# A fused attention and two-MoE kernel: later logits, transposes first, weight blocks and returning weights laid out and timed anew

## The chip, the cores and the metric

One core of a Trainium2 chip runs the whole program. The metric is the device time of one execution in microseconds (us); lower is better. The time before is the median of three runs.

## The reference, cut to what matters

Block-causal attention (8 batches, 8 heads, 576 positions, head size 64, blocks of 64) gives 4608 tokens of 512 numbers. They pass a first MoE layer (one expert, squared ReLU, 512 to 2048 to 512) and a second, soft one (32 slots).

```python
attn = softmax(where(block_i >= block_j, q @ k.T / 8, -1e9)) @ v
x = attn.transpose(0, 2, 1, 3).reshape(4608, 512)
h = np.maximum(x @ w_in, 0.0)             # 512 x 2048
x = h * h @ w_out                         # 2048 x 512
logits = x @ phi                          # 512 x 32
d = softmax over tokens(logits);  slot_input = d.T @ x
slot_out[e] = relu(slot_input[e] @ w1[e]) @ w2[e]      # 8 experts, 4 slots each
out = softmax over slots(logits) @ slot_out
```

## The kernel before, in words

**Chunks and slots.** The tokens are cut into 12 chunks of 384. The first MoE layer is cut into 16 blocks `ft` of 128 hidden columns. A slot is one chunk with one block: `slot_h` (line 885) makes the hidden values in the accumulator bank `HB` with 12 matmuls of 384 columns at line 899, and `slot_o` (line 912) adds their product with `w_out` into the three `O` banks with 9 matmuls of 512 columns at line 924. Each number is split into a high and a low part, so that three matmuls stand for one. There are 192 slots; chunk c covers the slots 16c to 16c+15 (chunks 0 and 1 share their slots in another order).

**Weights.** `W[ft]` holds the high part of a block, its first 512 columns of `w_in` and its last 512 of `w_out`. The low parts lie in DRAM (`wlo_d`) and come back through a ring of six tiles, `WL`, one 512 KB load a slot (line 890).

**Three fast stretches.** Chunks 4 and 5, 7 and 8, 9 and 10 are done in pairs by `fast` (line 1186). Sums and differences of the inputs (`combos`, line 1026, on VectorE and ScalarE) and of the weights let 7 products (`product`, line 1132, matmuls at line 1140) stand for 8. A fast stretch takes 32 slots: 8 pair loops over two blocks, each with 7 products and two `o_block` calls (line 1156, matmuls at 1168) for the second chunk's first half of the work, then a row of 16 `o_block` calls for the other chunk. The weight operands of the products pass through a ring in the first halves of `W[0]` to `W[7]`, filled by `w_entry` (line 1115); the combined inputs lie in `EX`, in the first halves of `W[8]` to `W[15]` and in `WL`. So after the first and the third fast stretch the first halves of all 16 `W` must return before chunks 6 and 11 are done in the plain way: line 1269 reads them from `whi_d`.

**Weight operands in DRAM.** Before the fast stretches, `prep` (line 1000) forms sums of the blocks for each of 8 pairs p, at the slots that `PREP` names (24 to 54), and stores their high and low parts in `ws_d` (lines 1022 and 1023), where a row of 512 numbers holds 256 of the high and 256 of the low part. Four of the seven operands are read from there (line 1128, one DMA). The other three are plain halves of blocks: line 1125 reads 128 KB from `whi_d`, line 1126 reads 128 KB from `wlo_d`, in rows of 1 KB. `whi_d` is written in the slots of chunk 2 (line 1471).

**The second layer's first half.** When a chunk's `O` banks close, they are copied to `X2`, and `moe2` (line 1280) runs for that chunk. For the 8 chunks numbered 2 to 9 in order of closing, VectorE transposes `X2` in 32x32 blocks into `XB` (line 1299), a DMA stores `XB` in DRAM (line 1302), and four DMAs read it back transposed into `YA` (line 1305). Then PE makes the logits (line 1331); a maximum, two exponentials, two small transposes (line 1361) and the product of the weights with `X2` (line 1384) follow, and the result is added into `acc`. `next(g_)` emits the part up to the DMAs when the chunk closes; the rest is emitted later, by `send(s)`, and its first matmul is tied to the first matmul of slot s (line 1334). That slot is the closing slot + 4 (lines 1193 and 1478). In a fast stretch's row of `o_block` calls, a slot number covers two calls.

**Attention.** Batches 0 and 1 are done at the start. For batches 2 to 7 `job64` (line 426) does two heads at a time, 24 jobs in all: scores in three phases (line 462), maxima on VectorE (472), exponentials on ScalarE (479), the joining of half rows (486 to 499), scaling (505, 506), transposes on VectorE (509), and the product with `v` (517, 72 matmuls). The jobs are spread over the slots by due times, `JOBS` (line 1435): first slot, and slots per job.

**What sets the order.** `Program.order` (line 99) is a planner: each step has costs, a due time and steps that it follows; a simulated clock picks, engine by engine, the ready step with the smallest due time, and the program is emitted in that order. `after` ties a step to others that must be placed before it. All DMAs go out on one queue, SP's, in that order; the queue stops at a DMA whose semaphores are not there yet. Four of the eight PSUM banks (`w`) are shared by attention, the odd products and the second layer.

Line 466 says when a job's first score matmul may be placed: after the factors (`fct`) of the job before are computed, so ahead of that job's product with `v`.

```python
after=() if i != ph_[0] else oldF + (fct_at if ph_ is PHASES[0] and fct_at else pv_end)
```

## Time and profile before

| | |
|---|---|
| median of three runs | 1192.55 us (1192.54 to 1194.65) |
| the profiled execution's own time | 1187.98 us |
| its span, first to last instruction | 1186.2 us |
| granted TensorE clock, mean | 0.989 |
| PE (matmul) busy | 1134.9 us, 96% |
| VectorE (DVE) busy | 864.6 us, 73% |
| ScalarE (ACT) busy | 641.4 us, 54% |
| DMA queue q1 | 259.54 MB, 67.2% of 16 engines |

Busy time is the time in which an engine had an instruction under way. Matmuls are pipelined, so a busy PE may still do less than it could; idle time of PE, and what ended it, is the more telling number. A row of the waits says which engine and line waited for which other, the total in us, how often, and the longest. A row of the timeline gives start and duration in us, then engine, line, operation and shape, merged over consecutive instructions of the same kind, and in brackets the idle time before it and what ended it. SPq is the DMA queue's own sequencer.

### The profile page before, as it was taken

The numbers are of one execution on the slowest core, as the hardware profiler recorded it, in microseconds if no ns is written. First come the engines' busy times: TensorE is split into PE (matmuls) and PEld (weight loads), VectorE is DVE, ScalarE is ACT, GpSimd is POOL, SyncE is SP. The second block draws the span as 40 slices with busy tenths as digits, with TensorE's granted clock in tenths as the row PEclk, the third lists the DMA queues.
The fourth block names the chain that finished last, engine by engine and source line by source line (L and its number), as shares of the span: only waits on it lengthen the run. The fifth ranks groups of instructions, "written<-read, shape, count | busy, mean of one in ns | idle before, by whom it ended". The sixth has DMA issues, their size and how long they took to land.

```text
span 1186.2 us, 28720 instructions
## 1 busy us (share of the span) xinstructions
PE 1134.9 (96%) x10918; PEld 931.5 (79%) x10918; DVE 864.6 (73%) x2469; ACT 641.4 (54%) x2041; POOL 4.1 (0%) x17
## 2 busy tenths in 40 slices
PE   5899999999999899999999999999999999899995
PEld 4677787878888788888877788788888899689843
DVE  7999988987778776887889777877896766532202
ACT  6888787667566466545566655646562000122324
POOL 1000000000000000000000000000000000000000
PEclk9899899999999999999999999999999999999998
DMA  7699547745555854665586653756564966997889
GB/s 232 200 340 292 179 154 265 242 166 184 183 180 186 251 173 138 189 198 179 173 261 238 218 177 95 224 187 192 179 185 140 292 206 191 360 374 249 295 329 320
DMA packets 145642, 261.37 MB, mean 220 GB/s; under 512 B 19680, under 2 KB 75232, under 8 KB 145504
## 3 DMA queue, kind: packets, MB, share of 16 engines
q1 hardware_dynamic: 145504, 259.54, 67.2%
q8 instruction: 86, 1.41, 0.5%
q14 instruction: 52, 0.43, 0.1%
HBM read 222.78 MB, written 36.70 MB: 219 GB/s over the span
## 4 chain that ended last, share of the span: by engine, by line
PE 77%; DVE 10%; DMA 7%; ACT 4%; issue 2%; SPq 0%; DVEq 0%; ACTq 0%
PE O L1168 16%; PE HB L899 14%; PE O L924 13%; PE HB L1140 9%; PE B L1140 6%; PE B L462 6%; PE B L517 5%; DMA WL<-wlo_d 3%; DMA YA<-xt_d 1%; PE B L1724 1%; DVE anm L645 1%; PE B L1331 1%; PE B L1384 1%; PE O L1688 1%; ACT aF L479 1%
## 5 line engine op out<-in xcount | busy, mean ns | idle before, releaser
L479 ACT ACTIVATE aF<-B,aF 128x192 f32<-128x192 f32 (+8 forms) x432 | 165.9, 418 | 51.5 <-DVE aF L474 38.3
L924 PE MATMUL O<-W,MG 128*128 128x512 f32 x600 | 178.1, 400 | 1.0 <-DVE MG L908 1.0
L1168 PE MATMUL O<-W,MG 128*128 128x512 f32 x576 | 167.8, 399 | 1.0 <-ACT X L1173 0.6
L899 PE MATMUL HB<-MX,W 128*128 128x384 f32 x544 | 148.8, 345 | 1.7 <-ACT R L905 1.7
L472 DVE TENSOR_REDUCE aF<-B 128x1 f32<-128x192 f32 (+8 forms) x432 | 109.7, 314 | 34.5 <-PE B L462 33.6
L924 PEld LDWEIGHTS O<-W,MG 128*128 128x128 f32 x600 | 110.2, 188 | 20.2 <-issue 1.9
L1168 PEld LDWEIGHTS O<-W,MG 128*128 128x128 f32 x576 | 106.0, 188 | 23.8 <-issue 1.7
L899 PEld LDWEIGHTS HB<-MX,W 128*128 128x128 f32 x544 | 98.6, 189 | 7.5 <-ACT R L905 2.6
L509 DVE STREAM_TRANSPOSE aF<-aF 128x256 f32<-128x256 f32 (+8 forms) x216 | 99.5, 490 | 0.0
L479 ACT ACTIVATION_READ_ACCUMULATOR aF<-B,aF 128x1 f32 x432 | 98.7, 230 | 0.0
L905 ACT ACTIVATE R<-HB 128x384 f32<-128x384 f32 x96 | 47.8, 498 | 86.1 <-PE HB L899 85.6
L1168 PE MATMUL O<-WL,MG 128*128 128x512 f32 x288 | 89.5, 398 | 0.3 <-DMA WL<-wlo_d 0.3
L924 PE MATMUL O<-WL,MG 128*128 128x512 f32 x264 | 78.9, 398 | 0.0
L899 PE MATMUL HB<-MX,WL 128*128 128x384 f32 x224 | 77.6, 346 | 0.4 <-DMA WL<-wlo_d 0.3
L462 PE MATMUL B<-aR 64*32 64x192 f32 (+8 forms) x3456 | 77.6, 302 | 0.0
L462 PEld LDWEIGHTS B<-aR 64*32 64x32 f32 x3456 | 53.6, 105 | 29.9 <-issue 7.8
L899 PE MATMUL HB<-MXe,W 128*128 128x384 f32 x256 | 72.0, 342 | 0.7 <-ACT R L905 0.6
L908 DVE CAST MG<-R 128x384 fp32r<-128x384 f32 x74 | 26.4, 357 | 57.1 <-ACT R L906 56.0
L517 PEld LDWEIGHTS B<-aF,aR 64*64 64x64 f32 x1728 | 53.2, 133 | 17.3 <-issue 4.9
L505 ACT ACTIVATE aF<-aF 128x256 f32<-128x256 f32 (+6 forms) x154 | 55.9, 437 | 18.4 <-DVE aF L499 18.2
L517 PE MATMUL B<-aF,aR 64*64 64x192 f32 (+8 forms) x1728 | 65.4, 301 | 0.0
L1168 PEld LDWEIGHTS O<-WL,MG 128*128 128x128 f32 x288 | 53.6, 188 | 14.1 <-DMA WL<-wlo_d 1.6
(365 smaller groups left out, 2190.6 us busy)
## 6 DMA issues: line engine op xcount, KB each, us to landing
WL<-wlo_d SPq DMA_DIRECT2D x83, 512.0 KB, 4.0
W<-ws_d SPq DMA_DIRECT2D x96, 256.0 KB, 3.2
WL<-wlo_d SPq DMA_DIRECT2D x96, 256.0 KB, 3.3
aR<-in_kq SPq DMA_DIRECT2D x24, 576.0 KB, 4.7
aR<-in_v SPq DMA_DIRECT2D x24, 576.0 KB, 3.8
W<-whi_d SPq DMA_DIRECT2D x72, 128.0 KB, 2.7
W<-wlo_d SPq DMA_DIRECT2D x72, 128.0 KB, 3.1
ws_d<-EX SPq DMA_DIRECT2D x16, 512.0 KB, 4.9
```

What stands on the lines that cost most here:

```text
L462: pe.matmul(bank(gs[h])[32 * g:32 * g + 32, c:c + 32 * i + 32].rearrange("p (b n) -> p b n", n=32), x[:, S + 64 * i + 32 * q_:S + 64 * i + ...
L472: pr.add(("dve", c_tt(n), lambda g=gs[h], n=n, c=c, x=x: dve.reduce_max(St[:, 0, x:x + 1], bank(g)[:, c:c + n], axis=AX.X, negate=True)), ...
L479: pr.add(("act", c_act(n, ext=2), lambda g=gs[h], n=n, c=c, x=x, i=i, h=h: act.activation(P_(i)[:, h], bank(g)[:, c:c + n], AF.Exp, bias=S ...
L505: act.activation(P_(i)[:, h], P_(i)[:, h], AF.Copy, scale=fct[:, x + h:x + h + 1])
L509: pr.add(("dve", c_tr(2 * n), lambda i=i: dve.transpose(P_(i), P_(i))), w=[K("P2", i, h) for h in range(2)])
L517: pe.matmul(bank(gs[q_])[64 * h:64 * h + 64, 32 * k:288].rearrange("p (i n) -> p i n", n=32), v_2()[sl, h, 64 * k:64 * k + 64], L0.F[sl, o ...
L899: pr.add(("pe", c_mm(CH), lambda a=a, b_=b_, sl=sl, n=n, k=k: pe.matmul(HB[:, 0:CH], (wl() if a == "l" else W[ft])[:, sl], b_(c, k), start ...
L905: pr.add(("act", c_act(CH), lambda: act.activation(r_, HB[:, 0:CH], AF.Relu)), w=["HB", ("r", j)], due=-1)
L908: pr.add([("dve", c_cp(CH), lambda: dve.tensor_copy(gh, r_)), ("act", c_act(CH, True), lambda: act.copy(gh, r_))], r=[("r", j)], w=[("gh", ...
L924: pr.add(("pe", c_mm(512), lambda a=a, b_=b_, sl=sl, t=t, p_=p_: pe.matmul(OB[t], a[:, sl], (wl() if b_ == "l" else W[ft])[:, 512:1024], s ...
L1140: pr.add(("pe", c_mm(CH), lambda a=a, b_=b_, k=k, fst=fst, lst=m == 5: pe.matmul((bank(g) if g else HB)[:, 0:CH], W[r][:, a + 128 * k:a + ...
L1168: pr.add(("pe", c_mm(512), lambda a=a, lo_=lo_, sl=sl, t=t, p_=p_: pe.matmul(OB[t], a[:, sl], wo(n) if lo_ else W[ft][:, 512:1024], start= ...
```

## The change

- `moe2`'s second half is sent at the closing slot + 6 in place of + 4 (lines 1195 and 1478).
- The 32x32 transposes of `X2` get the due time -1, ahead of everything that is ready on VectorE.
- `whi_d` is gone, with its 16 stores in chunk 2 (256 KB each). `ws_d` has 8 blocks a pair in place of 4. After `prep`'s own store, each of the two blocks of the pair is stored there too, high halves and low halves in rows of 512 numbers: two DMAs of 256 KB for each of 16 blocks. They read `W` and the slot's `WL` tile.
- `w_entry` reads all seven operands with one DMA of 256 KB, in rows of 2 KB.
- The returning first halves come from `ws_d`, in rows of 1 KB. Six go out beside `o_block` calls 8, 9, 11, 12, 14 and 15 of the last row; the other ten follow in slots 0 to 6 of the next chunk (6 and 11), two in slots 0, 3 and 6 and one in the others.
- In batches 2 and 3 a job's first score matmul is placed after the product with `v` of the job before; from batch 4 on as it was.
- `JOBS`: batch 4 takes 6 slots a job in place of 5.5; batch 5 starts at slot 78 in place of 76 and takes 6 in place of 5; batch 6 starts at 98 in place of 96 and takes 4.5 in place of 5; batch 7 takes 4.5 in place of 5.

```diff
-    whi_d = dram.tile([FT, 128, 512], F32, name="whi_d")
-    ws_d = dram.tile([FT // 2, 4, 128, 512], F32, name="ws_d")
+    ws_d = dram.tile([FT // 2, 8, 128, 512], F32, name="ws_d")
...
-                       after=() if i != ph_[0] else oldF + (fct_at if ph_ is PHASES[0] and fct_at else pv_end),
+                       after=() if i != ph_[0] else oldF + (fct_at if ph_ is PHASES[0] and fct_at and b > 3 else pv_end),
...
-        def put():
-            d_ = ws_d[p].rearrange("j p n -> p j n")
-            sp.dma_start(d_[:, :, 0:256], H_.rearrange("p (j n) -> p j n", j=4))
-            sp.dma_start(d_[:, :, 256:512], S_.rearrange("p (j n) -> p j n", j=4))
-        pr.add(("sp", 50, put), r=[("st", "S"), ("st", "H")], w=[("ws", p)], due=due, nbytes=1 << 20)
+        def put(j, n, *src):
+            d_ = ws_d[p, j:j + n].rearrange("j p n -> p j n")
+            for x, t in enumerate(src):
+                sp.dma_start(d_[:, :, 256 * x:256 * x + 256], t.rearrange("p (j n) -> p j n", j=n))
+        pr.add(("sp", 50, lambda: put(0, 4, H_, S_)), r=[("st", "S"), ("st", "H")], w=[("ws", p)], due=due, nbytes=1 << 20)
+        for y, ft in enumerate((e, o)):
+            wl, lk = lo(s + y)
+            pr.add(("sp", 50, lambda y=y, ft=ft, wl=wl: put(4 + 2 * y, 2, f(W[ft][:, 0:512]), f(wl()[:, 0:512]))),
+                   r=[("W", ft, 0), lk + (0,)], w=[("wa", ft)], due=due, nbytes=1 << 19)
...
         def go():
-            d_ = f(W[r])
-            if j in (1, 2, 4):
-                ft, c0 = (o if j == 4 else e), (0 if j == 1 else 256)
-                sp.dma_start(d_[:, 0:256], whi_d[ft][:, c0:c0 + 256])
-                sp.dma_start(d_[:, 256:512], wlo_d[ft][:, c0:c0 + 256])
-            else:
-                sp.dma_start(d_[:, 0:512], ws_d[p, {5: 0, 6: 1, 7: 2, 3: 3}[j]])
-        pr.add(("sp", 50, go), r=[("wh", e), ("wh", o), ("wd", e), ("wd", o), ("ws", p)], w=[("W", r, 0)], due=due, nbytes=1 << 18)
+            sp.dma_start(f(W[r])[:, 0:512], ws_d[p, {5: 0, 6: 1, 7: 2, 3: 3, 1: 4, 2: 5, 4: 7}[j]])
+        pr.add(("sp", 50, go), r=[("wa", e), ("wa", o), ("ws", p)], w=[("W", r, 0)], due=due, nbytes=1 << 18)
...
+    def reload(ft, due, after):
+        pr.add(("sp", 50, lambda: sp.dma_start(
+            f(W[ft])[:, 0:512].rearrange("p (j n) -> p j n", j=2),
+            ws_d[ft // 2, 4 + 2 * (ft % 2):6 + 2 * (ft % 2)].rearrange("j p n -> p j n")[:, :, 0:256])), r=[("wa", ft)], w=[("W", ft, 0)],
+               due=due, nbytes=1 << 18, after=idle(XW_KEYS[ft]) + [after])
...
-            return s + 4, g_
+            return s + 6, g_
...
-            for ft in range(FT):
-                pr.add(("sp", 50, lambda ft=ft: sp.dma_start(f(W[ft])[:, 0:512], whi_d[ft])), r=[("wh", ft)], w=[("W", ft, 0)],
-                       due=t_at(s) + 2.5 * ft, nbytes=1 << 18, after=idle(XW_KEYS[ft]) + [at_b[ft]])
+            for ft in range(6):
+                reload(ft, t_at(s) + 2.5 * ft, at_b[8 + ft * 3 // 2])
...
-                    r=[("X2", t)], w=[("a", "XB", t)], due=due, after=oldF)
+                    r=[("X2", t)], w=[("a", "XB", t)], due=-1, after=oldF)
...
-    JOBS = {2: (10, 5.5), 3: (32, 5.5), 4: (54, 5.5), 5: (76, 5), 6: (96, 5), 7: (116, 5)}
+    JOBS = {2: (10, 5.5), 3: (32, 5.5), 4: (54, 6), 5: (78, 6), 6: (98, 4.5), 7: (116, 4.5)}
...
+        if after_fast(c) and ft < 7:
+            for x in range(6, FT):
+                if (x - 6) * 3 // 4 == ft:
+                    reload(x, t_at(s) - 5, h_at[s - 1])
         slot_h(s, t_at(s), () if s else swapped)
-        if c == 2:
-            pr.add(("sp", 50, lambda ft=ft: sp.dma_start(whi_d[ft], f(W[ft])[:, 0:512])), r=[("W", ft, 0)], w=[("wh", ft)],
-                   due=t_at(s) + 2, nbytes=1 << 18)
...
-            part = (s + 4, g_)
+            part = (s + 6, g_)
```

## Rows read from the trace of the kernel before

**Rows 1.** The profile's page: busy us of each engine, share of the span, instructions.

```profile
PE 1134.9 (96%) x10918; PEld 931.5 (79%) x10918; DVE 864.6 (73%) x2469; ACT 641.4 (54%) x2041; POOL 4.1 (0%) x17
```

**Rows 2.** Waits of PE, 235 to 1125 us: total us, times, longest.

```profile
PE B L1331 <- DMA YA<-xt_d: 5.6, 2, 3.2
PE B L1140 <- ACT aF L479: 1.9, 1, 1.9
...
PE B L1361 <- ACT LE L1346: 0.3, 1, 0.3
```

**Rows 3.** Timeline of PE, 398 to 408 us (chunk 3 under way).

```profile
406.07 1.07 PE L1331 MATMUL B<-YA,ph 128*32 128x128 f32 x24 [3.23 <-DMA YA<-xt_d]
```

**Rows 4.** Timeline of PE, 1003 to 1056 us (the last row of o_block calls).

```profile
1030.08 1.07 PE L1331 MATMUL B<-YA,ph 128*32 128x128 f32 x24 [2.41 <-DMA YA<-xt_d]
...
1033.83 1.06 PE L1384 MATMUL B<-X,ET 128*32 128x512 f32 x6
```

**Rows 5.** Timeline of SP, the DMA queue, 352 to 412 us.

```profile
390.59 0.39 SPq L1302 DMA_DIRECT2D xt_d<-aF  x1
...
395.63 2.85 SPq L1305 DMA_DIRECT2D YA<-xt_d  x4
```

**Rows 6.** Timeline of SP, 1000 to 1050 us.

```profile
1011.55 0.37 SPq L1302 DMA_DIRECT2D xt_d<-aF  x1
...
1019.98 2.33 SPq L1305 DMA_DIRECT2D YA<-xt_d  x4
```

**Rows 7.** Busy by stretch: PE, PEld, DVE, ACT, POOL, clock, DMA share, GB/s.

```profile
1005.00:1050.00 45.00, 41.89 (x211) 32.75 (x211) 21.60 (x52) 7.71 (x20) 0.00 (x0) 1.00 1.05 374
```

**Rows 8.** DMA issues of the whole run: count, KB each, median us to landing.

```profile
W<-ws_d SPq DMA_DIRECT2D x96, 256.0 KB, 3.2
...
W<-whi_d SPq DMA_DIRECT2D x72, 128.0 KB, 2.7
...
ws_d<-EX SPq DMA_DIRECT2D x16, 512.0 KB, 4.9
W<-whi_d SPq DMA_DIRECT2D x32, 256.0 KB, 6.5
```

**Rows 9.** The chain that ended last, in order of time: start us, us, what.

```profile
234.43 2.64 PE B L517 x72
...
263.60 2.64 PE B L517 x72
...
437.83 2.64 PE B L517 x72
...
693.94 2.27 PE O L924 x9
...
698.32 2.09 PE O L924 x9
...
1000.44 2.09 PE O L1168 x9
...
1058.72 2.10 PE HB L899 x12
```

**Rows 10.** Timeline of DVE, 478 to 485 us (chunk 3 closes, first fast stretch begins).

```profile
480.32 1.89 DVE L1299 STREAM_TRANSPOSE aF<-X 128x512 f32<-128x512 f32 x3
482.13 0.52 DVE L1222 TENSOR_TENSOR MXe<-HB,R 128x384 f32<-128x384 f32 x1
```

**Rows 11.** Timeline of PE, 478 to 485 us, the same place.

```profile
482.70 0.61 PE L1140 MATMUL HB<-W,W 128*128 128x384 f32 x2 [1.04 <-DVE MXe L1222]
```

**Rows 12.** Timeline of DVE, 1005 to 1012 us (a chunk closes in the last fast stretch).

```profile
1007.02 1.40 DVE L1299 STREAM_TRANSPOSE aF<-X 128x512 f32<-128x512 f32 x2 [0.76 <-ACT X L1173]
...
1010.82 0.70 DVE L1299 STREAM_TRANSPOSE aF<-X 128x512 f32<-128x512 f32 x1
```

**Rows 13.** Timeline of PE, 233 to 268 us: a job's first scores right behind a product.

```profile
237.00 1.09 PE L462 MATMUL B<-aR 64*32 64x288 f32 x32
```

**Rows 14.** Waits of SP's queue, 280 to 440 us: total us, times, longest.

```profile
SPq L890 <- PE O L924: 62.0, 25, 5.0
```

## The prediction

> **What bounds the kernel now.** The page's first part comes first: PE is busy in 96% of the span, VectorE in 73%, ScalarE in 54% [rows 1]. So PE sets the time, and only what PE waits for, or what it does in addition, can move it. Up to about 235 us the program stays as it is: the first job whose placing changes starts there, and all stores that move come later. So I read the waits of PE from 235 to 1125 us, where the tail begins. They are ten rows, from 5.6 down to 0.3 us, 11.4 us together [rows 2]. That is nearly all that better placing can win: under 1% of the run.
>
> The largest row, 5.6 us in two waits, is PE at the first logits matmul (L1331), waiting for the transposed copy `YA`. The timeline of PE shows the places: 3.23 us ending at 406.07, for the chunk closed before slot 48 [rows 3], and 2.41 us ending at 1030.08, in the last row of `o_block` calls [rows 4]. PE runs its list in order, so all that stands behind that matmul waits too. The queue's timeline says why `YA` is late. At the first place the store went out at 390.59 and the loads 5.0 us later [rows 5]; at the second, at 1011.55 and 8.4 us later [rows 6]. That second stretch, 1005 to 1050, has the DMA engines full: share 1.05, 374 GB/s [rows 7]. The sixteen returning weights are in it, 256 KB each, and the median of that kind over the run is 6.5 us to landing [rows 8].
>
> **The change, part by part.** *Logits two slots later.* In a plain chunk two slots are two times 12 matmuls of 384 columns (2.10 us) and 9 of 512 (2.09 us), 8.4 us [rows 9]. In a row of `o_block` calls they are four calls of 2.09 us, again 8.4 us [rows 9]. The waits were 3.2 and 2.4 us, so `YA` is there with 5.2 and 6.0 us to spare. For three of the eight chunks with a DMA transpose (those that close at slots 64, 112 and 144) nothing moves, since the pair loop sends only every third slot and meets +4 and +6 at the same pair; both waits are among the other five. Late next would be the emptying of the `O` banks into `X2`, which must wait until L1384 has read the old `X2`. From logits to L1384's end that took 4.8 us [rows 4], and calls 12 to 15 last 8.4 us, so it is covered by 3.6 us; if not, PE would wait for the rest of a chain of 4.8 us. Term: -5.6 us; ends 0 (another wait steps in) and -5.6.
>
> *Returning weights spread.* Ten of sixteen leave the full stretch and go out in slots 0 to 6 of the next chunk, each some six slots, 25 us at 4.2 us each [rows 9], before its use, against 6.5 us to landing [rows 8]. That takes 2.6 MB, about 7 us at 374 GB/s [rows 7], out of the stretch. It helps the same second wait, which is already counted. Rows are 1 KB where they were 2 KB; the nearest row with 1 KB is 128 KB in 2.7 us [rows 8], so two such in turn, 5.4 us, stay far inside 25 us. Term: 0; without the cover, one landing of 6.5 us.
>
> *Transposes first.* VectorE's work is the same. In five of the eight chunks the three transposes already stand in one run, and one of these shows the cost: three in 1.89 us stand ahead of the addition that frees `HB` [rows 10], and PE waits 1.04 us for that addition [rows 11]. In the other three chunks they are split [rows 12]; there they will now close up ahead of other work. Three chunks times 0 to 1.04 us gives 0 to +3.1; a gain is excluded once `YA` has time to spare. As the splits run one call ahead, I take one such wait: +1.0 us.
>
> *First scores behind the product, batches 2 and 3.* Six jobs change (in the second one the scores already came right behind, at 237.00 after the product at 234.43 [rows 13, 9]). PE then goes from one small-tile form to the next without the large tiles between. Nine matmuls right after such scores took 2.27 us in place of 2.09 [rows 9]: 0.18 us saved a job, six times 1.1. I take -1.0; ends 0 and -1.1. The jobs may also become longer, which is a rival below.
>
> *Weight blocks in one piece.* 72 DMAs fewer on SP's queue (240 become 168), and the operand comes in one DMA with 3.2 us to landing in place of two of 128 KB [rows 8]. None of the ten rows that make the 11.4 us is a wait for `W` [rows 2], so there is nothing to win: 0. The cover is that an entry is due nearly three slots ahead; without it each late one costs up to 3.2 us.
>
> *Stores.* Sixteen of 256 KB leave chunk 2 and 32 of 256 KB come in at the slots of `prep`. They move 4 MB more, and each pair holds a `WL` tile until it has read it. PE does not wait for them: 0, while the six tiles of the ring give five slots of lead; the rival on the queue has the price.
>
> *Attention dues.* The same PE work at other places: 0. The nearest row is PE waiting 1.9 us for exponentials that hold a bank [rows 2]; that may go or come again, -1.9 to +1.9. More generally the planner places everything after 235 us anew, so the other waits, 11.4 less 5.6, may lie anywhere from gone to doubled: -5.8 to +5.8. I take 0, for lack of a sign.
>
> **Sum.** -5.6 + 1.0 - 1.0 = -5.6 us. The profiled execution took 1187.98 us, of which 1186.2 are span; it gives 1182.4. The median of the runs lies 4.57 us above that execution, and I carry that over: **1187.0 us**.
>
> **The rivals.** *More falls away.* The same, and most of the other 5.8 us of waits goes in the new order: 4 us more, 1183.0. For it: the changed dues lie where several of these waits are. Against: nothing aims at them. Chance 0.12.
>
> *Given back.* PE goes on without its pause, and VectorE, 73% busy over the run [rows 1] and also serving attention, becomes the late one: the 3.2 us come back as waits for splits, and a transposes' wait of 1.0 us comes with them, so that only 2.4 less 1.0 remain: 1191.1. For it: VectorE is late by a microsecond at a chunk's close [rows 10, 11]. Against: waits of PE for VectorE are small elsewhere. Chance 0.20.
>
> *Attention late: slower.* Batches 2 and 3 run their jobs one behind another. Place: the first fast stretch, whose combined inputs need the last job of batch 3. Price: the first of the eight products began at 234.43, the last at 437.83 [rows 9], seven steps of 29.1 us; the one step that already ran in the new order, to 263.60, took 29.2 [rows 9]. So at the old pace nothing is lost. The fast stretch went on at 482.70 [rows 11], 44.9 us after that last product; it decides from 6.4 us more a job. At 8 us more PE would stand some 11 us: 1198. Chance 0.10.
>
> *The queue stands behind the new stores: slower.* A load that refills a `WL` tile must wait for the store that still reads it, and everything behind it on SP's queue waits too. A store into `ws_d` takes 4.9 us to land [rows 8]. But that queue already stands 62 us out of 160, in 25 waits for the `O` matmul that frees the tile [rows 14], and PE does not notice. It decides where about four stores in a row, 20 us, eat the lead of five slots, 21 us. Two waits of 4.9 us reaching PE would give 1196.8. Chance 0.04. The Trainium skill, page "DMA: Bandwidth & Descriptors", section on the anatomy of one DMA, speaks for this rival: a semaphore wait sits on the issuing sequencer before dispatch, and the receipt of a write is slowest when it goes to HBM; by that page alone the new stores would be a cost and the sum the 1196.8, by the rows it is 1187.0, since a standing queue has cost PE nothing so far.
>
> **How the numbers follow.** About 0.2%, 2.4 us, is what a measurement of this kernel can tell from no change. The forecast has 0.54, so faster has 0.54 + 0.12 = 0.66, no change 0.20, slower 0.10 + 0.04 = 0.14. The range goes from 1182.0, the forecast with nearly all other waits gone (5.0 of 5.8 us), to 1193.5, past the case in which the gain is given back; what is left out is the two slower rivals and a little below, under 2 in 10.
>
> **What would show it.** In the changed kernel: no wait of PE for `YA` at the logits; the three transposes of every chunk in one run; 168 DMAs of 256 KB from `ws_d` into `W` for the operands and none from `whi_d`; the DMA share from 1005 to 1050 well under 1.05; the eighth product of attention near 438 us; waits of PE from 235 to 1125 us of about 7 us in all. Wrong would be: a new row of waits for VectorE of over 3 us, a wait for `WL` in 290 to 430 us, or a first fast stretch that starts later than 483 us.

## The result, and the profile after

The changed kernel takes 1180.65 us (median of six runs, 1179.87 to 1183.47) beside 1193.76 us for the kernel before, measured with it: ratio 0.9885 [0.9856, 0.9914]. The forecast was 1187.0 us with a range from 1182.0, so the direction was right and the gain of 13.1 us was more than twice the 5.6 us forecast. Two repeats on other chips gave 0.9916 [0.9896, 0.9937] and 0.9910 [0.9891, 0.9930]. Over all three the median is 1183.1 us in 18 executions, against 1194.9 in 94 of the kernel before: 11.8 us.

The profiled executions stand closer: 1179.87 against 1187.98, 8.1 us. The page of the changed kernel, its busy line (answers to [rows 1]) and four of its DMA issues:

```profile
PE 1130.9 (96%) x10918; PEld 930.9 (79%) x10918; DVE 862.0 (73%) x2464; ACT 642.0 (54%) x2047; POOL 4.1 (0%) x17
...
W<-ws_d SPq DMA_DIRECT2D x200, 256.0 KB, 3.3
...
ws_d<-EX SPq DMA_DIRECT2D x16, 512.0 KB, 5.8
ws_d<-W SPq DMA_DIRECT2D x16, 256.0 KB, 5.1
ws_d<-WL SPq DMA_DIRECT2D x16, 256.0 KB, 3.7
```

Operands (168) and returning halves (32) now have one form. The stores of `prep` into `ws_d` land later than in [rows 8], 5.8 against 4.9 us. PE is busy 4.0 us less here, but 1137.3 and 1134.6 us in the profiles of the two repeats: the sum over the whole run changes with the clock at the start, so it is compared below from the first product of attention on.

Waits of PE, 235 to 1125 us, the changed kernel (total us, times, longest; answers to [rows 2]):

```profile
PE HB L1137 <- DVE MXe L1225: 1.7, 2, 1.1
PE HB L898 <- ACT R L904: 0.7, 2, 0.5
PE B L1654 <- DVE acc L1391: 0.6, 1, 0.6
PE O L1165 <- DVE MG L1149: 0.5, 1, 0.5
PE B L1363 <- ACT LE L1348: 0.3, 1, 0.3
PE B L1314 <- DVE X L929: 0.2, 1, 0.2
```

These make 4.0 us where there were 11.4. Both waits for `YA` are gone, as forecast; so are the 1.9 us for exponentials and most of the small ones. The two logits, on the timeline of PE (start, us, what; brackets would show a wait; answers to [rows 3, 4]):

```profile
414.83 1.07 PE L1333 MATMUL B<-YA,ph 128*32 128x128 f32 x24
...
1041.98 1.07 PE L1333 MATMUL B<-YA,ph 128*32 128x128 f32 x24
```

The stretch 1005 to 1050 (busy PE, PEld, DVE, ACT, POOL, clock, DMA share, GB/s; answers to [rows 7]):

```profile
1005.00:1050.00 45.00, 44.65 (x246) 34.65 (x247) 23.15 (x63) 8.80 (x25) 0.00 (x0) 1.00 1.02 362
```

PE is busy 44.65 us of 45 in place of 41.89, yet the DMA engines are nearly as full as before: 1.02 against 1.05. The prediction's sign that this share would lie well under 1.05 did not come.

Attention, on the chain and on the timeline of PE (answers to [rows 9, 13]):

```profile
265.28 2.64 PE B L516 x72
267.92 1.02 PE B L461 x32
```

```profile
437.48 2.71 PE L516 MATMUL B<-aF,aR 64*64 64x288 f32 x72
```

On the timeline of PE a job's scores stand right behind a product at six places in batches 2 and 3, where there was one. The eighth product still begins at 437.5, so the jobs did not get longer. The close of chunk 3, on the timelines of DVE and of PE (answers to [rows 10, 11]):

```profile
476.38 1.89 DVE L1301 STREAM_TRANSPOSE aF<-X 128x512 f32<-128x512 f32 x3
478.20 0.52 DVE L1225 TENSOR_TENSOR MXe<-HB,R 128x384 f32<-128x384 f32 x1
```

```profile
478.77 0.62 PE L1137 MATMUL HB<-W,W 128*128 128x384 f32 x2 [1.14 <-DVE MXe L1225]
...
741.18 0.62 PE L1137 MATMUL HB<-W,W 128*128 128x384 f32 x2 [0.54 <-DVE MXe L1225]
```

The first wait behind three transposes is there as before, 1.14 against 1.04 us; the second, at the start of the second fast stretch, is new. The three chunks whose transposes were split are split still (at 598, 861 and 1001 us), so that sign did not come either.

The start of the program takes a different time in every execution. So the profiles are best compared from the first product of attention to the end: length, then busy us of PE, for two profiles of the kernel before and three of the changed one (two of them are the repeats below).

```profile
234.43:1186.20 951.77, 926.64 (x9534) 761.59 (x9533) 652.31 (x1866) 452.72 (x1541) 0.00 (x0) 0.99 0.67 216
237.31:1192.38 955.07, 929.57 (x9533) 764.82 (x9533) 652.51 (x1866) 452.40 (x1541) 0.00 (x0) 0.99 0.67 215
```

```profile
235.66:1178.09 942.43, 924.36 (x9534) 762.75 (x9533) 649.57 (x1860) 453.57 (x1548) 0.00 (x0) 0.99 0.70 226
238.01:1181.33 943.32, 924.77 (x9534) 762.71 (x9533) 649.63 (x1860) 454.07 (x1548) 0.00 (x0) 0.99 0.70 226
241.40:1185.66 944.26, 924.98 (x9533) 762.79 (x9533) 649.45 (x1860) 454.09 (x1548) 0.00 (x0) 0.99 0.70 225
```

In the pair that the prediction is about this part is 9.3 us shorter: PE is idle 7.1 us less and busy 2.3 us less, and the start came 1.2 us later, which leaves the 8.1 us. What is open is why the medians lie 11.8 us apart, and which part removed which wait.

### The profile page after: what moved, and what is told of

It reads as the page before. It is cut to its first block, busy times and chain, and to the rows that moved or that the text cites. A ratio compares the mean times of both kernels' runs of the same rounds, so it can differ in the third digit from the quotient of the medians.

```text
span 1178.1 us, 28641 instructions
## 1 busy us (share of the span) xinstructions
PE 1130.9 (96%) x10918; PEld 930.9 (79%) x10918; DVE 862.0 (73%) x2464; ACT 642.0 (54%) x2047; POOL 4.1 (0%) x17
## 4 chain that ended last, share of the span: by engine, by line
PE 79%; DVE 7%; ACT 3%; DMA 3%; issue 1%; SPq 0%; DVEq 0%; ACTq 0%
PE O L1165 17%; PE HB L898 13%; PE O L923 13%; PE HB L1137 9%; PE B L1137 6%; PE B L461 6%; PE B L516 5%; PE B L1727 1%; PE B L1333 1%; ACT aF L478 1%; PE B L1386 1%; PE O L1691 1%; PE B L726 1%; PE B L753 1%; DVE anm L644 1%
## 5 line engine op out<-in xcount | busy, mean ns | idle before, releaser
L898 PEld LDWEIGHTS HB<-MX,W 128*128 128x128 f32 x544 | 98.3, 189 | 13.1 <-ACT R L904 5.5
L508 DVE STREAM_TRANSPOSE aF<-aF 128x448 f32<-128x448 f32 (+8 forms) x216 | 98.4, 488 | 0.0
L904 ACT ACTIVATE R<-HB 128x384 f32<-128x384 f32 x96 | 47.6, 496 | 83.7 <-PE HB L898 80.9
L504 ACT ACTIVATE aF<-aF 128x256 f32<-128x256 f32 (+8 forms) x162 | 58.7, 432 | 19.3 <-DVE aF L498 19.3
L516 PEld LDWEIGHTS B<-aF,aR 64*64 64x64 f32 x1728 | 52.8, 133 | 17.3 <-issue 4.7
```

The costliest lines, as they stand in the source:

```text
L504: act.activation(P_(i)[:, h], P_(i)[:, h], AF.Copy, scale=fct[:, x + h:x + h + 1])
L508: pr.add(("dve", c_tr(2 * n), lambda i=i: dve.transpose(P_(i), P_(i))), w=[K("P2", i, h) for h in range(2)])
L516: pe.matmul(bank(gs[q_])[64 * h:64 * h + 64, 32 * k:288].rearrange("p (i n) -> p i n", n=32), v_2()[sl, h, 64 * k:64 * k + 64], L0.F[sl, o ...
L898: pr.add(("pe", c_mm(CH), lambda a=a, b_=b_, sl=sl, n=n, k=k: pe.matmul(HB[:, 0:CH], (wl() if a == "l" else W[ft])[:, sl], b_(c, k), start ...
L904: pr.add(("act", c_act(CH), lambda: act.activation(r_, HB[:, 0:CH], AF.Relu)), w=["HB", ("r", j)], due=-1)
```

## The experiments

The main theory is that a wait of PE costs more than its length, as the granted clock can fall behind it, so that the kernel before runs mostly above the one execution that was profiled. Its rivals: a wait costs its length, and the rest comes from the attention dues, or from the weights. Ratios are to the kernel before measured beside each run; in brackets behind a time stands the number of executions. Several experiments were measured without the changed kernel beside them; they are compared with it through their ratios, and that is said.

### The kernel before, once more

No edit; twelve executions.

> The kernel before, unchanged, measured as if it were a change. Ratio 1.000 by every theory. The question is the gap between its profiled execution (1187.98 us) and its median (1193.76 us). Theory A (a wait that varies): the executions differ by how long PE waits for the transposed copy; its runs spread over 1188 to 1200 us, and where a run is slow its granted clock is below 0.989 or its wait at the first logits row is longer than 3.2 us. Theory B (chance): the profiled execution was a lucky one of a spread that has nothing to do with the changed parts; then this profile shows the same two waits, 3.2 and 2.4 us, and a time anywhere between 1188 and 1202 us.

Ratio 1.0016 [0.9996, 1.0036]. Its profiled execution took 1194.16 us. Waits of PE, 235 to 1125 us, then the timeline of PE at the first logits:

```profile
PE B L1331 <- DMA YA<-xt_d: 3.0, 1, 3.0
PE B L1331 <- DMA W<-whi_d: 2.9, 1, 2.9
PE B L1140 <- ACT aF L479: 1.9, 1, 1.9
```

```profile
408.76 1.07 PE L1331 MATMUL B<-YA,ph 128*32 128x128 f32 x24 [3.00 <-DMA YA<-xt_d]
...
410.91 0.84 PE L899 MATMUL HB<-MX,W 128*128 128x384 f32 x2
```

and two stretches of the same execution (the last three columns: clock, DMA share, GB/s):

```profile
409.00:415.00 6.00, 6.00 (x44) 4.93 (x37) 3.71 (x13) 2.66 (x8) 0.00 (x0) 0.72 0.30 106
752.00:765.00 13.00, 11.14 (x112) 10.37 (x111) 9.20 (x29) 7.94 (x34) 0.00 (x0) 0.87 0.93 257
```

A clock of 0.72 over 6 us is 3.4 us at the lower level of 1.2 GHz, which costs 1.7 us; 0.87 over 13 us, behind the wait of 1.9 us, is the same again. The third long wait, the 2.9 us at the second logits, had no such piece behind it. Two matmuls of 384 columns take 0.84 us at the lower level, and 0.51 at 2.4 GHz. In the execution on which the prediction rests, the same two places show 1.00:

```profile
400.00:420.00 20.00, 16.77 (x217) 12.57 (x223) 13.28 (x41) 7.89 (x25) 0.00 (x0) 1.00 0.81 222
752.00:765.00 13.00, 11.12 (x59) 9.93 (x59) 9.85 (x32) 10.71 (x42) 0.00 (x0) 1.00 1.04 314
```

The rest of the 6.2 us between the two was lost earlier: the chain of the repeat puts the first product of attention at 237.31, not at 234.43.

```profile
237.31 2.64 PE B L517 x72
```

2.9 us and twice 1.7 us make 6.3 us. All 94 further executions of this kernel took longer than the profiled one (the fastest 1188.38 us), so the profile that the prediction read was the luckiest of 95. The waits at the logits were much the same in the slower execution, as theory B had it, but its clock was lower, which theory A named.

### Logits alone, and logits back

Before, with the later logits only:

```diff
-            return s + 4, g_
+            return s + 6, g_
...
-            part = (s + 4, g_)
+            part = (s + 6, g_)
```

> Before, with the logits at the closing slot + 6 and nothing else changed. Theory A (the two waits for the transposed copy are the main part, and in most executions they cost more than in the profiled one): both rows of PE waiting for the copy vanish, 5.6 us or more less than before in time, ratio 0.990 to 0.995. Theory B (the gain is in the other parts and in the new order): at most 0.997. Theory C (given back elsewhere): the rows vanish, and as much waiting comes up at other lines; ratio 0.998 to 1.001.

1191.28 us (12), 0.9957 [0.9942, 0.9972]: 5.1 us of gain. The longest waits of its profile:

```profile
PE HB L899 <- ACT R L905: 2.0, 3, 1.1
...
PE HB L1140 <- DMA W<-ws_d: 1.8, 1, 1.8
```

`YA` is gone from the list, and other waits stepped in, 11.3 us in all, none above 1.9. That is as much waiting as before, in shorter pieces: by the waits this is theory C, by the time theory B. From the first product to the end the profile took 954.1 us, no less than the kernel before (951.8 and 955.1). The mean clock is higher than beside it (0.9855 against 0.9825), but where the 5.1 us of the medians were won this one trace does not show.

The changed kernel, with the logits at +4 again (the reverse edit):

> The changed kernel with the logits back at the closing slot + 4. Theory A: the wait at chunk 2's logits returns with about 3 us, the one in the last row returns smaller (under 2.4 us, since ten weights no longer load there); ratio to before 0.993 to 0.996. Theory B: no more than 1.5 us slower than the changed kernel, ratio 0.988 to 0.990.

1184.92 us (6), 0.9913 [0.9891, 0.9936]. One wait comes back, and the clock falls behind it:

```profile
PE B L1333 <- DMA YA<-xt_d: 2.1, 1, 2.1
...
409.00:415.00 6.00, 5.18 (x39) 4.06 (x43) 3.45 (x12) 0.90 (x4) 0.00 (x0) 0.72 0.96 348
```

At the second place no wait returned. With the weights laid out anew, +4 is late once only, so the parts overlap. The ratio fits neither theory. The time is 1.8 us above the changed kernel's median, which was measured on other chips, and the intervals overlap; the trace gives a wait of 2.1 us and 1.7 us of clock, and 946.1 us from the first product to the end in place of 942.4 to 944.3. So the later logits are worth some 2 to 4 us in the new kernel, against 5.1 in the old one.

### The wait filled with matmuls

Before, with ten matmuls whose result nobody reads ahead of the logits of the two late chunks:

```diff
+        for x in range(10 if c in (2, 9) else 0):
+            pr.add(("pe", 231, lambda g=g: pe.matmul(bank(g), W[0][:, 512:640], W[0][:, 512:1024], start=True, stop=True)),
...
```

> Before, with ten idle matmuls of 512 columns (2.3 us of work whose result nobody reads) right ahead of the logits of chunk 2 and of chunk 9, the two places where PE waits for the transposed copy. Nothing is taken away. Theory A (a wait of some 3 us lets the granted clock of TensorE fall to half for 3.4 us in most executions, and that is the part of the 13 us which the waits themselves do not explain): the waits shrink by about 2.3 us each, the clock stays at 1.00 behind them, the mean granted clock over the runs rises from 0.982 to about 0.984, and the time falls by 1.5 to 3 us although work was added: ratio 0.9975 to 0.9990. Theory B (the clock has no part in it): ratio 1.000, or up to 1.002 where the copy comes early.

1198.49 us (12), 1.0037 [1.0020, 1.0053]: slower, where the theory of the clock wanted a gain. The timeline of PE at the first place:

```profile
405.12 2.45 PE L1326 MATMUL B<-W 128*128 128x512 f32 x10
408.63 1.07 PE L1334 MATMUL B<-YA,ph 128*32 128x128 f32 x24 [1.06 <-DMA YA<-xt_d]
```

The clock held here, but the logits started no earlier than in the repeat, the step behind them waited 1.15 us more, and in all the waits for `YA` were still 4.4 us, 3.3 of them at the second place, where the clock held too. It fell behind the 1.9 us for exponentials instead (0.89 from 750 to 765 us). Both theories missed the time, and the mean clock did not rise (0.9825 against 0.9836 beside it). This test does not decide: it added work and waits of its own.

### Waiting given in a dose

The changed kernel, with ten further copies on ScalarE in each of five slots of chunk 11, and the square in that chunk on ScalarE alone, so that five hidden blocks come late:

```diff
+        def sq_():
+            act.activation(r_, r_, AF.Square)
+            for _ in range(10 if c == 11 and ft % 3 == 1 else 0):
+                act.activation(r_, r_, AF.Copy)
...
```

> The changed kernel with ten copies more on ScalarE (0.5 us each, the same numbers over themselves) in each of the slots 1, 4, 7, 10 and 13 of chunk 11, where neither attention nor the second layer stands between: each should make PE wait some 3 us once, five times in all, and nothing else. It measures the price of such a wait. Theory A (the clock falls behind some of them): 15 us of waits, and for each stretch of 3.4 us at half clock 1.7 us more; pieces of half clock in that stretch of the profile, a mean granted clock 0.001 to 0.006 lower than that of the changed kernel, 16 to 23 us slower. Theory B (no part of the clock): 15 us slower, no piece of half clock there, the same mean clock.

1206.46 us (6), 1.0105 [1.0080, 1.0130]; the changed kernel beside it took 1183.8, so the dose costs 22.7 us. The waits of PE and the timeline behind one of them:

```profile
PE O L927 <- DVE MG L911: 11.6, 4, 2.9
```

```profile
1078.69 0.96 PE L927 MATMUL O<-W,MG 128*128 128x512 f32 x3 [2.90 <-DVE MG L911]
...
1080.39 1.48 PE L927 MATMUL O<-W,MG 128*128 128x512 f32 x3
```

and a stretch around each of the five (a fifth wait of 2.90 us ends at 1130.55):

```profile
1059.00:1067.00 8.00, 6.81 (x20) 5.94 (x21) 1.82 (x4) 1.61 (x4) 0.00 (x0) 0.57 0.52 168
1078.00:1085.00 7.00, 6.31 (x23) 5.62 (x24) 1.75 (x4) 1.40 (x4) 0.00 (x0) 0.76 0.56 175
1096.00:1101.00 5.00, 5.00 (x17) 4.35 (x18) 1.39 (x3) 0.46 (x1) 0.00 (x0) 0.66 0.34 107
1113.00:1118.00 5.00, 4.74 (x15) 4.04 (x16) 1.60 (x4) 0.72 (x2) 0.00 (x0) 0.66 0.06 7
1130.00:1135.00 5.00, 4.45 (x14) 3.58 (x15) 1.75 (x4) 1.27 (x4) 0.00 (x0) 0.66 0.20 41
```

In this execution the clock fell at all five. Length times what is missing of the clock, 8 x 0.43 + 7 x 0.24 + 3 x 5 x 0.34, makes 10.2 us; with the 14.5 us of waiting that is 24.7. From the first product to the end this profile took 967.6 us, 24.3 more than the mean of the changed kernel's three. The waits alone would have been 14.5. The profiled execution was the slowest of the six; by the medians a wait of 2.9 us costs 4.5 us, by the profile 4.9. For these waits this decides for the clock: theory A.

### The attention dues

Before, with the new table `JOBS` and the new rule for the first scores, nothing else:

```diff
-    after=() if i != ph_[0] else oldF + (fct_at if ph_ is PHASES[0] and fct_at else pv_end),
+    after=() if i != ph_[0] else oldF + (fct_at if ph_ is PHASES[0] and fct_at and b > 3 else pv_end),
...
-    JOBS = {2: (10, 5.5), 3: (32, 5.5), 4: (54, 5.5), 5: (76, 5), 6: (96, 5), 7: (116, 5)}
+    JOBS = {2: (10, 5.5), 3: (32, 5.5), 4: (54, 6), 5: (78, 6), 6: (98, 4.5), 7: (116, 4.5)}
```

> Before, with the other due times of attention and with the first scores behind the product in batches 2 and 3, nothing else. Theory A: 1.0 us saved by joined small-tile work, and the other waits by chance; ratio 0.997 to 1.002, both waits for the transposed copy stay. Theory B: this part carries what the logits do not, 5 us or more; ratio 0.993 to 0.996.

1191.52 us (12), 0.9975 [0.9954, 0.9997]: 3.0 us. The waits for `YA` stay (5.3 us), the 1.9 us at the shared bank go. Undone together on the changed kernel (the reverse edit):

> The changed kernel with the old due times of attention and the old rule for a job's first scores. Theory A (this part gives the 3 us that it gave alone): 2.5 to 3.5 us slower than the changed kernel, ratio to before 0.990 to 0.992, with the wait of an odd product for an exponential (1.9 us) back. Theory B (it only reshuffles): ratio 0.987 to 0.990, as the changed kernel.

1189.07 us (12), 0.9959 [0.9945, 0.9973]. The changed kernel was not measured beside it; against its three ratios, 0.9885 to 0.9916, this is 5 to 9 us slower, more than either theory allowed. From the first product to the end it took 949.3 us, 5.0 to 6.9 more than the changed kernel. Then each half on the changed kernel. The old table alone:

> The changed kernel with the old table of due times, but the first scores of batches 2 and 3 still behind the product. With both undone the time was 8 us longer in the profile. Theory A (the table does it: it moves the job whose exponentials hold the bank at the start of the second fast stretch): 4 us or more slower than the changed kernel, the 1.9 us wait at an odd product back. Theory B (the rule for the first scores does it, by joined small-tile work and fewer held banks): within 2 us of the changed kernel.

1184.53 us (6), 0.9921 [0.9899, 0.9942], against 0.9916 for the changed kernel beside it: 0.7 us, which this measurement cannot tell from nothing (theory B). Its trace shows what the table does, though: the wait for the bank is back.

```profile
PE B L1137 <- ACT aF L478: 1.9, 1, 1.9
```

The old rule alone (`b > 3` taken out):

> The changed kernel with the old rule for a job's first scores in batches 2 and 3, and the new table of due times. The old table alone cost 0.7 us (1184.53 by 1183.80), both undone cost 8 us in the profile. Theory A (rule and table are worth what they are worth together, so the rule carries most): 3 to 6 us slower than the changed kernel. Theory B (two orders that differ by chance): within 2 us of it.

1186.14 us (6), 0.9934 [0.9920, 0.9949], against 0.9910 for the changed kernel beside it: 2.9 us by the ratios, with intervals that just overlap. The row of its waits that grew, and its row from the first product to the end:

```profile
PE HB L898 <- ACT R L904: 2.1, 3, 1.4
```

```profile
235.53:1182.28 946.75, 927.05 (x9533) 761.75 (x9533) 649.72 (x1863) 451.60 (x1542) 0.00 (x0) 0.99 0.70 225
```

With the scores ahead of the product, PE waits 1.4 us more in all for ScalarE, which empties `HB` at L904 and also makes the exponentials. And the same matmuls keep PE busy 2.3 us longer, 927.05 in place of 924.4 to 925.0 us. So of the attention part the rule is the half that can be measured. The two halves make 3.6 us and both together 5 or more; that rest is not explained.

### The weights

Before, with the blocks of `ws_d`, their stores and the returning weights, and nothing else:

```diff
-    whi_d = dram.tile([FT, 128, 512], F32, name="whi_d")
+    ws_d = dram.tile([FT // 2, 8, 128, 512], F32, name="ws_d")
...
+            sp.dma_start(f(W[r])[:, 0:512], ws_d[p, {5: 0, 6: 1, 7: 2, 3: 3, 1: 4, 2: 5, 4: 7}[j]])
...
+            for ft in range(6):
+                reload(ft, t_at(s) + 2.5 * ft, at_b[8 + ft * 3 // 2])
```

> Before, with the weight blocks and the returning weights of the changed kernel alone (one store more, rows of 2 KB, six returns in the last row and ten in the next chunk); logits, transposes and attention as before. Theory A: the wait at chunk 2's logits stays with 3 us, the second one in the last row falls below 1 us: 2 to 4 us less, ratio 0.9965 to 0.9985. Theory B (blocks of 2 KB and spreading matter nothing while PE sets the time): 0.999 to 1.001, both waits as they were.

1190.77 us (12), 0.9970 [0.9951, 0.9989]: 3.6 us, as theory A had it. Of the two waits for `YA` the first is left with 1.8 us; the second, in the last row, is gone, and a new one of 2.4 us for ScalarE has come:

```profile
PE HB L1137 <- ACT aF L504: 2.4, 1, 2.4
...
PE B L1333 <- DMA YA<-xt_d: 1.8, 1, 1.8
```

The changed kernel, with all sixteen returning weights in the last row again, measured twice:

```diff
-            for ft in range(6):
-                reload(ft, t_at(s) + 2.5 * ft, at_b[8 + ft * 3 // 2])
+            for ft in range(FT):
+                reload(ft, t_at(s) + 2.5 * ft, at_b[ft])
...
-        if after_fast(c) and ft < 7:
+        if False and after_fast(c) and ft < 7:
```

> The changed kernel with all sixteen returning weights issued beside the sixteen calls of the last row again, from the new blocks. Theory A: with the logits two slots later the copy has time to spare, so no wait for it comes back and the time is that of the changed kernel within 1 us, ratio 0.988 to 0.990; the DMA share from 1000 to 1045 us is over 1.0 again. Theory B (the spread is needed): PE waits for the copy or for a low-part tile by 2 us or more in the last row, ratio 0.990 or more.

> The changed kernel with all sixteen returning weights in the last row. Its profile lay 3.3 us above that of the changed kernel, its median 6 us above that of another call. Theory A (two low-part tiles late by 0.9 us together and a fuller DMA, worth 2 to 4 us): ratio to before 0.992 to 0.994. Theory B (the 6 us were of the call): within 1.5 us of the changed kernel.

1187.07 us (8), 0.9946 [0.9925, 0.9968], and 1184.41 (6), 0.9923 [0.9908, 0.9937] beside 0.9910 for the changed kernel: 1.5 us, the same sign twice, though these last two intervals overlap. Its profiles wait for `WL`, 0.9 us in one and 1.7 in the other; the first of them, and the stretch 1000 to 1045 without and with the spread:

```profile
PE O L1165 <- DMA WL<-wlo_d: 0.9, 2, 0.5
...
1000.00:1045.00 45.00, 43.45 (x228) 33.36 (x229) 21.51 (x52) 7.94 (x19) 0.00 (x0) 1.00 1.06 372
```

```profile
1000.00:1045.00 45.00, 44.14 (x242) 34.58 (x241) 22.00 (x56) 9.45 (x25) 0.00 (x0) 1.00 1.02 362
```

The spread lowers the share by 0.04 only. Nor does it keep the loads of `WL` from coming late in every execution: with it, one of the changed kernel's three profiles waits 0.7 us for such a load in the same row. From the first product to the end the two profiles without the spread took 944.2 and 943.5 us, no more than those with it (942.4 to 944.3). So a gain of the spread is not shown here. No wait for `YA` returns without it: with logits at +6 `YA` has room in the full stretch too.

### Transposes back

The changed kernel, with the old due time, twice:

```diff
-                    r=[("X2", t)], w=[("a", "XB", t)], due=-1, after=oldF)
+                    r=[("X2", t)], w=[("a", "XB", t)], due=due, after=oldF)
```

> The changed kernel with the transposes of a chunk at their old due time. Theory A (they cost PE about as much as they save, and the copy has time to spare): within 1.5 us of the changed kernel, either side. Theory B (they carry part of the gain): 2 us or more slower, with a wait for the transposed copy or for a bank that the changed kernel does not have.

> The changed kernel with the transposes at their old due time, which was 1.6 us below the changed kernel in the call before, less than the runs' spread. Theory A (the transposes ahead of all else cost about 1 us, as the forecast had it): 0.5 to 2 us below the changed kernel again. Theory B (no effect): within 0.5 us of it.

1182.17 us (6), 0.9904 [0.9881, 0.9927], and 1182.29 (6), 0.9906 [0.9892, 0.9920], beside 0.9916 and 0.9910: the medians lie 1.6 and 0.2 us lower, which is within their intervals. The traces lean the same way. Both wait 3.1 us in all, the changed kernel 4.0 to 5.2, and from the first product to the end they took 941.9 and 941.6 us against 942.4 to 944.3. So the transposes ahead of all else gain nothing here and may cost about a microsecond. The two repeats of the changed kernel that served as the measure:

> The changed kernel once more, for twice the runs. Theory A (waits of PE of about 2 us and more let the granted clock fall in part of the executions; the kernel before has three of these after 235 us, the changed one none): mean granted clock 0.985 to 0.987 against 0.982 to 0.984 before, ratio 0.987 to 0.991, of which 7 to 8 us are waits and 2 to 4 us clock. Theory B (the first six runs were lucky): ratio 0.992 to 0.994, as the profiled executions put it (1179.87 by 1187.98), and equal clocks.

> The changed kernel beside the three variants of this call. By the twelve runs so far: ratio to before 0.988 to 0.992, mean granted clock 0.984 to 0.986.

The first repeat's ratio, 0.9916, lies between its two theories, and its mean clock was that of theory B: 0.9830 beside 0.9838 for the kernel before, no gain where theory A wanted some 0.003. The second came as expected: 0.9910, and a clock of 0.9847 beside 0.9832.

### The clock over all runs

Mean granted clock, and (1 - clock) times the median, by kernel:

| kernel | longest wait, us | mean clock | lost to the clock, us |
|---|---|---|---|
| before, 94 executions | 3.0 to 3.2 | 0.9829 | 20.4 |
| before, dues only | 2.7 | 0.9831 | 20.2 |
| before, wait filled | 3.3 | 0.9825 | 21.0 |
| before, logits only | 1.9 | 0.9855 | 17.3 |
| before, weights only | 2.4 | 0.9849 | 18.0 |
| changed, dues back | 1.9 | 0.9853 | 17.4 |
| changed, 18 executions | 1.1 | 0.9847 | 18.1 |
| changed, with the dose | 2.9, five times | 0.9773 | 27.3 |

Much of each loss lies at the start and in the tail, and at the start it differs between executions of one kernel. In the changed kernel's profile 7% of the first 72 us is lost, in that of its first repeat 16%, 5.0 against 11.5 us (the last three columns: clock, DMA share, GB/s):

```profile
0.00:72.00 72.00, 51.51 (x333) 41.11 (x334) 62.91 (x196) 55.18 (x147) 4.08 (x17) 0.93 0.71 228
```

```profile
0.00:72.00 72.00, 53.56 (x319) 42.55 (x320) 61.98 (x194) 53.38 (x143) 4.10 (x17) 0.84 0.70 226
```

In single executions this scatter is larger than the effect sought. Its 2.3 us between the kernel before and the changed one is an estimate, and its two parts that can be checked side by side disagree: -0.8 and +2.0 us in the two repeats. The traces answer it directly, by the stretch from the first product of attention to the end. The waits are those of its first 890 us, the pieces at half clock those before the tail:

| kernel, by its profiles | first product, us | from there to the end, us | waits of PE, us | pieces at half clock |
|---|---|---|---|---|
| before, two | 234.4, 237.3 | 951.8, 955.1 | 11.4, 11.8 | none, two |
| before, logits only | 236.6 | 954.1 | 11.3 | none |
| before, dues only | 237.7 | 951.1 | 9.7 | one |
| before, weights only | 239.4 | 951.1 | 9.8 | none |
| changed, three | 235.7, 238.0, 241.4 | 942.4, 943.3, 944.3 | 4.0, 4.1, 5.2 | none |

Between the means of the first and the last line lie 10.1 us. Of these 6.7 us are idle time of PE, 1.7 the clock (3.4 us over two profiles), and the rest, 1.7 us, a shorter busy time of the same matmuls. So the waits are the main cause and the clock behind them a small part. The 11.8 us of the medians hold 1.7 us more, which lie in the start or in executions without a trace and stay open. Taken one by one, the three parts bring little in this stretch, at most 2.3 us each against the mean of the first line, though by their ratios they gain 5.1, 3.0 and 3.6 us. So the sizes of the single parts are less sure than the whole.

## Why the prediction was right and wrong

**The step that failed most is the last of the sum**: the offset of 4.57 us between the profiled execution and the median, carried over as a constant. In the result it was 0.8 us (1180.65 less 1179.87). That is 3.8 of the 6.3 us by which the forecast was high. The profiled execution of the kernel before was the fastest of 95 and the only trace looked at; in it no wait cost any clock, while the second profile lost 3.4 us behind two of them. The changed kernel has no such wait, and none of its three profiles loses clock in that stretch. Over all executions the offset is 6.9 us for the kernel before (1194.9 less 1187.98) and 3.3 us for the changed one (1183.1 less 1179.87). Of this difference about 2 us are the clock behind the long waits, as an estimate from the traces and the means; the rest may be luck of the start, which the runs do not settle.

**The other 2.5 us are in the terms.** In the pair of profiles idle time of PE fell by 7.1 us where -5.6 + 1.0 = -4.6 was forecast, and its busy time by 2.3 where 1.0 was; the start gave 1.2 back.

**Logits, -5.6: right.** Both waits went, and nothing late took their place: no wait for the emptying of `O` into `X2`. But the term does not belong to the logits alone: the weights, without them, also remove the second wait and leave 1.8 us of the first.

**Returning weights, 0 because "already counted": right as far as the runs show.** It does help the second logits wait. The 1.5 us by which the spread looks better in the medians is not in the traces. The 7 us of transfers taken out of the stretch lowered its share by 0.03 to 0.04 only.

**Transposes, +1.0: too large in the profile, and for another reason.** The three split chunks, on which the term rested, stayed split. The new wait is 0.54 us, at a chunk whose transposes already stood in one run; undoing this part removes 1 to 2 us of waits.

**First scores behind the product, -1.0: too small.** The price of 0.18 us a join came from one pair of rows. Undone on the changed kernel, this part costs 2.3 us of busy time and 1.4 us of waits for `HB`, 2.9 us by the ratios. The waits for `HB` are no part of what was gained over the kernel before, where that row was 0.6 us. **Attention dues, 0 (±1.9): right as a bound.** The 1.9 us wait went; in time that is 0.7 us, not clear of noise.

**Other waits, 0 "for lack of a sign": wrong.** The 5.8 us that were not `YA`'s became 4.0. That is part of the rival "more falls away", whose 1183.0, with a chance of 0.12, came nearest.

**The rivals.** *Given back*: the largest row for VectorE is 1.7 us, refuted. *Attention late*: eighth product at 437.5, refuted. *The queue behind the new stores*: no profile of the changed kernel waits for a load of `WL` between 290 and 430 us, refuted. The Trainium skill, page "DMA: Bandwidth & Descriptors", section on the anatomy of one DMA, spoke for this rival; it describes DMAs issued by GpSimd, and here all go out on SP's queue. The rows agree that writes into DRAM are slow to land: the stores of 256 KB into `ws_d` took 5.1 us from `W` and 3.7 from `WL`, loads of that size from `ws_d` 3.3. That this costs PE anything no row here shows.

## What to carry to other kernels

When PE is busy 96%, list its longest waits first and take them away whole: each costs its length and, in some executions, a piece at half clock behind it. Before adding up savings against one profiled execution, compare its time and mean clock with those of many runs: if it is the fastest, the sum has to start from the typical one. When the start of a program scatters, compare traces from a fixed step on. Undo each part of a bundle as well as adding it alone: here the attention part gives 3.0 us alone and costs 5 or more when undone, and the logits go the other way.

## What the chip showed that was not expected

A long wait of PE was followed by a slow clock in some executions and not in others. Without the dose, the traces of this case hold 17 waits of 1.83 to 3.34 us after the first product; at five of them the clock fell to 1.2 GHz for 3.4 us (waits of 3.0 and 1.9 us in the repeat of the kernel before, 2.1 with the logits back, 2.6 with the dues only, 1.9 with the wait filled). At twelve it did not, among them 3.23 us at 406.07 and 2.41 at 1030.08 [rows 3, 4] and the longest, 3.34. With the dose it fell at five of five waits of 2.90 us. What decides is open. A piece costs 1.7 us, half its length. The Trainium skill, page "TensorE: Matmul & The Clock Gate", section "HAM oscillation — how this bites in real kernels", counts the price of throttled time as half of it, and the dose agrees: 24.7 us by that count against 24.3 measured in the same execution.

The start of the program differs from one execution to the next: the first product of attention begins at 234.4 and 237.3 us in two executions of the kernel before, and at 235.7, 238.0 and 241.4 us in three of the changed one.
